# Later transposing DMAs and row stores, earlier operand fetches, and paused rest splits in an attention and SwiGLU kernel

## The chip, the cores and the metric

The kernel runs on one core of one Trainium2 chip. The metric is the device time of one execution in microseconds. Matrix products run on TensorE (PE in the profile; PEld are its weight loads), elementwise work on VectorE (DVE), ScalarE (ACT) and GpSimd (POOL). Every DMA of this kernel is issued by SyncE (SP), one after the other, in the order in which the program names them.

## The reference, cut to what matters

For one sequence of 2048 tokens with 576 channels the kernel computes an attention `a` with a memory (32 heads of 18 channels, four segments of 512 tokens), a SwiGLU feed-forward network `b` with 4608 hidden channels, and a gate that mixes them:

```python
g = _sigmoid((x * gate_w).sum(-1, keepdims=True))
# attention, for each segment of 512 tokens and each head
p = _softmax(qs @ ks.T * scale + mask)
a_dot = p @ vs
a_mem = (phi(qs) @ M) / (phi(qs) @ z + 1e-6)
o = sig_beta * a_mem + (1.0 - sig_beta) * a_dot
M, z = M + phi(ks).T @ vs, z + phi(ks).sum(0)
a = o @ wo
# feed-forward network
b = (_silu(x @ w_gate) * (x @ w_up)) @ w_down
return g * a + (1 - g) * b
```

## The kernel before

**Stages.** A first stage projects queries, keys and values and updates the memory. Then comes the long stage that the change touches: the feed-forward network, with the attention's scores and products woven between its matmuls. A last stage applies `wo` and the gate.

**The feed-forward stage** has two halves of 1024 tokens. Each half runs over 36 tiles `f` of 128 hidden channels. A tile takes seven products of two-term operands (`seven`, L1289 for the 512 main channels, L1292 for the 64 rest channels), which are combined into gate and up values by a scheme of sums of blocks (L1360 to L1386, on ScalarE and VectorE). The first half makes the weights' two-term operands itself (`w_make`), stores them to `wc`, and the second half fetches them (`w_fetch`, L805) in four operand pairs: products 0 and 3, 1 and 2, 4 and 5, and 6. Each pair goes into one of eight buffers. The rest channels' weight rows lie in `rc`; `r_block` makes them in the first half for later tiles (load L293, four sums on GpSimd L284 to L287, high term L294, low term L276, three stores L291), and `r_fetch` (L298) fetches a tile's rows. After every third tile the hidden values of three tiles are multiplied by `w_down` in 16 groups (L1074, sums L1083) during the next tile. Their down weights are loaded (`draw`, L260), split (L1055, L1056) and stored in the first half, and fetched (L1062) in the second.

**Beats.** A tile has eight beats, 0 to 7, each called by `tick()` behind one of the products (beats 5 and 6 together behind the sixth). `defer(k, fn)` puts a function into a later beat's list, so that it is emitted k beats on; an entry `(o, fn)` of a tile's plan is emitted in beat `o` of that tile, and with `o` of 8 or more in the next tile. The attention is a generator (`att_gen`) that is advanced by a credit: some beats emit one or two of its steps, called ticks (`tau`) here. Between the halves stand ten more beats (`BREAK`) in which the last 16 groups of the first half run. All of it is one fixed program order; on each engine the instructions run in that order, and an instruction that waits holds up what stands behind it.

**The attention** works in 64 units of two heads and one segment; a unit has five score banks, one for each tick, `u, n = divmod(tau, 5)`. The stacked queries and keys of the next unit are loaded in ticks n = 2 (six DMAs) and n = 3 (four DMAs, L1009). Odd units, and all early ones, compute a second, transposed set of scores (`t_bank`, L943). In the second half even units are "turned": the scores of one orientation are exponentiated (`e_bank`, TURN[0] ticks behind), split into two terms (`c_bank`, TURN[1] ticks behind: cast on VectorE L886, subtraction on GpSimd L887), transposed by a DMA (`turn`, TURN[2] ticks behind, L891) and multiplied with the values (`pv_turned`, TURN[3] ticks behind, L903 and L904). The terms and the transposed blocks have six places each, used in turn.

**The second half's inputs.** `x_second` and `rest_second` make the operands of the other 1024 tokens late in the first half. `rest_second` belongs to the last tile of the first half (`pos` 35) and the beats after it: two loads of two tiles each (L1245), sums on GpSimd (L1250), high terms on ScalarE (L1257) and low terms on VectorE (L1261).

Of the kernel before, what the change touches and what calls it, by code (L numbers as in the profile page):

```python
# [12 lines left out]
F32 = mybir.dt.float32  # L13
F32R = mybir.dt.float32r
BF = mybir.dt.bfloat16
F16 = mybir.dt.float16
I32 = mybir.dt.int32
AF = mybir.ActivationFunctionType
# [3 lines left out]
P = 128  # L22
# [17 lines left out]
TL = 12  # L40
PL = 2
VL = 3
TURN = (1, 3, 7, 17)
HALF = ((2, 3), (0, 1))
TICK = ((0.0, 1.0), (0.76, 1.0))
QUIET = (5, 6)
# [3 lines left out]
FIRST = (9, 10, 15, 17)  # L50
# [17 lines left out]
def gated_mix(ctx, tc, xT, xrest, wf, wfr, wfh, wd, wv, wo, beta, cmask, ident, bmask, out):  # L68
    nc = tc.nc
# [31 lines left out]
    one, sx = sc[:, ONE:ONE + 1], sc[:, SX:SX + 1]  # L101
    sw = [sc[:, SW + i:SW + i + 1] for i in range(FT // 4)]
    iw = [sc[:, IW + i:IW + i + 1] for i in range(FT // 4)]
    xo = pool(ctx, "xo", 1)
# [73 lines left out]
    def xr_tile(j):  # L178
        return xo.tile([P, L], F32, name=f"xr{j}")
# [94 lines left out]
    def rest_low(t, a, i):  # L274
        t, a = (z.rearrange("p j n -> p (j n)") for z in (t, a))
        nc.vector.scalar_tensor_tensor(t, a, sw[i], t, op0=OP.mult, op1=OP.subtract)  # L276

    def r_block(h, o):
        i, c = divmod(h, 2)
        a = rp.tile([P, 7, 64], F32, name="rr", bufs=1)  # L280
        t = rp.tile([P, 8, 64], F16, name="rt", bufs=1)[:, :7]

        def sums():
            nc.gpsimd.tensor_sub(a[:, 5], a[:, 0], a[:, 1])  # L284
            nc.gpsimd.tensor_add(a[:, 1], a[:, 1], a[:, 3])
            nc.gpsimd.tensor_sub(a[:, 4], a[:, 1], a[:, 0])
            nc.gpsimd.tensor_sub(a[:, 6], a[:, 2], a[:, 4])  # L287

        def keep(k):
            d = rc[i, 32 * k:32 * k + 32].rearrange("r f (j n) -> (r f) j n", n=P)  # L290
            nc.sync.dma_start(d[:, :, 64 * c:64 * c + 64], t)  # L291

        return [(o, lambda: nc.sync.dma_start(a[:, 0:4], wfh[h - 4])), (o + 2, sums),  # L293
                (o + 3, lambda: nc.scalar.activation(t, a, AF.Copy, scale=sw[i])), (o + 3, lambda: keep(0)), (o + 3, lambda: keep(1)),  # L294
                (o + 4, lambda: rest_low(t, a, i)), (o + 5, lambda: keep(2))]

    def r_fetch(f):
        nc.sync.dma_start(rhs[f % 2][:96].rearrange("p j n -> p (j n)"), rc[f // 4, :, f % 4])  # L298
# [38 lines left out]
    with ExitStack() as st:  # L337
# [245 lines left out]
        rr = {}  # L583
# [88 lines left out]
        for s in range(NSEG):  # L672
# [52 lines left out]
            if s == 3:  # L725
                qst_.close()
                rp = pool(ctx, "rp", 4, side="right")
# [13 lines left out]
            for n in range(8):  # L741
                hf, i = divmod(n, 4)
# [41 lines left out]
    with ExitStack() as st:  # L784
# [15 lines left out]
        def w_fetch(f):  # L800
            ops = wops[1, f] = [None] * 7

            def one(k):
                t, _ = op_pair(ops, k)
                nc.sync.dma_start(t, wc[f, k, :, :t.shape[1]])  # L805

            return [((2, 3, 6, 8)[k] if f else FIRST[k], lambda k=k: one(k)) for k in range(4)]

        kp = pool(ast, "kp", 2, side="right")
        ap = pool(ast, "ap", 2, side="right")  # L810
# [428 lines left out]
        def rest_second(rest):  # L1239
            rr = {}  # L1240

            def load(b):
                for a in range(2):
                    rr[b, a] = raw_tile()
                    nc.sync.dma_start(rr[b, a], xrest[HALF[1][b]][:, a])  # L1245

            def total(j):
                c, d, e, g = rr[0, 0], rr[1, 0], rr[0, 1], rr[1, 1]
                o, p, q = {1: (c, d, c), 4: (d, g, d), 2: (g, g, c), 6: (e, e, g)}[j]
                nc.gpsimd.tensor_sub(o, p, q)  # L1250

            def source(j):
                return rr[((0, 0), (0, 0), (1, 1), (0, 1), (1, 0), (1, 1), (0, 1))[j]]

            def high(j):
                rest[j] = xr_home(1, j)
                nc.scalar.activation(rest[j], source(j), AF.Copy, scale=sx)  # L1257

            def low(j):
                t = rest[j][32:64]  # L1260
                nc.vector.scalar_tensor_tensor(t, source(j)[32:64], sx[32:64], t, op0=OP.mult, op1=OP.subtract)  # L1261

            todo = [(0, load, 0), (2, high, 0), (2, high, 3), (3, low, 0), (3, low, 3), (4, load, 1), (6, high, 5),
                    (6, total, 1), (7, low, 5), (7, high, 1), (8, total, 4), (8, low, 1), (9, total, 2), (9, high, 4),
                    (10, low, 4), (11, total, 6), (11, high, 2), (12, low, 2), (13, high, 6), (14, low, 6)]
            return [(o, lambda fn=fn, j=j: fn(j)) for o, fn, j in todo]

        def glance(i, k):
# [28 lines left out]
        for pos, (half, f) in enumerate(seq):  # L1297
# [6 lines left out]
            plan = []  # L1304
            if nxt:
                plan += w_make(nxt[1]) if nxt[0] == 0 else w_fetch(nxt[1])
                plan.append((1 if nxt[1] else 10, lambda f=nxt[1]: r_fetch(f)))
                for n, h in enumerate(BLOCKS.get(pos, ())):
                    plan += r_block(h, 4 * n)
                if half == 0 and f + 2 < FT:  # L1310
                    wraw_of[f + 2] = [None, None]
                    for u in range(2):
                        plan.append(((2, 5)[u], lambda u=u, f=f: wraw_of[f + 2].__setitem__(u, w_load(f + 2, u))))
            i = 1 + pos // 3
# [8 lines left out]
                second = x_second(X2, 0) + x_second(X2, 1)  # L1323
            if 24 <= pos <= 33 and pos % 3 == 0:
                plan += second.pop(0)
            if pos == 35:
                XR2 = [None] * 7
                plan += rest_second(XR2)
            for o, fn in plan:
                defer(o + 1, fn)  # L1330
            step = [0]
# [96 lines left out]
        for n in range(17):  # L1428
# [6 lines left out]
            if n:  # L1435
                tt = order[n - 1]
                ff = ffs.pop(n - 1)
                for hf in range(2):
                    c = slice(288 * hf, 288 * hf + 288)
                    t = chain_tile()  # L1440
# [67 lines left out]
```

## Time and profile before

| what | value |
|---|---|
| median of 3 runs | 1770.49 us (1768.05 to 1770.83) |
| the profiled execution | 1773.57 us |
| its span, first to last instruction | 1771.9 us |
| mean granted TensorE clock | 0.995 |
| TensorE busy, share of the span | 97% |
| VectorE, ScalarE, GpSimd busy | 75%, 58%, 48% |
| moved by DMA | 314.77 MB |

In the rows of the profile, a group reads: line, engine, operation, output<-input, count, busy time and mean duration in ns, and the idle time of the engine before them with what ended it. A wait row reads: who waited, for whom, total us, times, longest. A timeline row reads: start, duration (us), engine, line, operation, operands. SP's rows show how long the issue of a DMA took, not how long its data moved. The halves of the feed-forward stage run from about 235 to 943 us and from there to about 1690 us; a tile without groups takes some 12 to 15 us, one with groups some 33 us.

### The profile page before, as it was taken

What the parts mean: (1) busy time and instruction counts of PE and PEld (TensorE: products, weight loads), DVE (VectorE), ACT (ScalarE), POOL (GpSimd) and SP (SyncE); (2) the same over time, 40 slices, a digit from 0 to 9 for tenths busy, and PEclk for the clock granted to TensorE, in tenths of its full rate; (3) what the DMA queues carried; (4) which work ended last, traced back from release to release, by engine and by line L of the source; (5) the groups of instructions that cost most, each with busy time, mean ns of one, the idle gap of its engine ahead of it and who ended that gap; (6) DMA issues with size and microseconds to landing.
All of it is one profiled execution on the core that took longest, in us unless ns stands there. A gap on an engine that the chain in (4) does not pass through costs nothing.

```text
span 1771.9 us, 35305 instructions
## 1 busy us (share of the span) xinstructions
PE 1721.6 (97%) x12241; PEld 1219.3 (69%) x12241; DVE 1322.9 (75%) x3239; ACT 1025.3 (58%) x1800; POOL 841.8 (48%) x1065
## 2 busy tenths in 40 slices
PE   9999999999999999999989999999999999999999
PEld 7888856656766676567656756756756766766699
DVE  6778776778878878888886878778767687775455
ACT  7656575667676666655654565556456365464411
POOL 3334551345535554656442755556546464553121
PEclk9999999999999999999999999999999999999999
DMA  8655475676677666545444477676566678664544
GB/s 284 226 192 175 143 256 193 210 225 193 172 244 223 199 186 190 188 143 156 164 159 164 108 184 166 143 184 173 137 170 167 134 174 179 154 157 138 172 140 141
DMA packets 330986, 314.77 MB, mean 178 GB/s; under 512 B 190644, under 2 KB 247860, under 8 KB 330808
## 3 DMA queue, kind: packets, MB, share of 16 engines
q1 hardware_dynamic: 330808, 312.52, 61.0%
q8 instruction: 97, 1.59, 0.4%
q14 instruction: 81, 0.66, 0.1%
HBM read 188.51 MB, written 97.69 MB: 162 GB/s over the span
## 4 chain that ended last, share of the span: by engine, by line
PE 75%; DVE 8%; DMA 5%; ACT 5%; issue 3%; SPq 3%; POOL 2%; DVEq 0%; ACTq 0%; POOLq 0%
PE bank L1289 29%; PE bank L1074 22%; PE bank L171 8%; PE bank L1292 5%; PE bank L830 3%; PE bank L943 2%; PE bank L971 1%; SPq L1009 1%; DMA draw<-in_wd_dram 1%; PE bank L973 1%; DMA rc<-rt 1%; PE bank L903 1%; DMA kst<-stk 1%; DVE junk L848 1%; DVE xo L1227 1%
## 5 line engine op out<-in xcount | busy, mean ns | idle before, releaser
L1074 PE MATMUL bank<-dw,hh 128*128 128x320 f32 (+1 forms) x2304 | 510.2, 314 | 8.4 <-DVE ya L1083 6.3
L1074 PEld LDWEIGHTS bank<-dw,hh 128*128 128x128 f32 x2304 | 380.5, 190 | 33.7 <-DVE ya L1083 9.7
L1074 PE MATMUL bank<-dw,hl 128*128 128x320 f32 (+1 forms) x1152 | 340.9, 296 | 3.4 <-DVE hl L124 3.4
L1043 POOL TENSOR_TENSOR p<-pe,p 128x512 f16<-128x512 f32 x220 | 272.7, 1240 | 86.3 <-DVE p L1041 64.2
L947 ACT ACTIVATE pe<-bank 128x512 f32<-128x512 f32 x220 | 130.5, 593 | 223.0 <-PE bank L943 198.7
L1083 DVE TENSOR_TENSOR ya<-bank,ya 128x320 f32<-128x320 f32 x352 | 157.6, 453 | 102.6 <-PE bank L1074 100.5
L1074 PEld LDWEIGHTS bank<-dw,hl 128*128 128x128 f32 x1152 | 218.5, 190 | 3.9 <-DVE hl L124 3.9
L955 POOL TENSOR_SCALAR_AFFINE_SELECT pe<-pe 128x256 f32<-128x256 f32 (+1 forms) x220 | 90.5, 412 | 216.5 <-ACT pe L947 205.5
L1292 PE MATMUL bank<-xr,rh 128*128 128x512 f16 x504 | 191.8, 381 | 0.0
L848 DVE CUSTOM_DVE_ANT_0 junk<-bank,cm 128x128 bf16<-128x128 f32 (+2 forms) x352 | 170.1, 483 | 17.8 <-PE bank L830 12.7
L312 POOL TENSOR_TENSOR ws<-raw 128x256 f32<-128x256 f32 x72 | 67.1, 932 | 154.5 <-DMA raw<-in_wf_dram 94.5
L830 PE MATMUL bank<-kst,qst 108*128 108x512 bf16 (+3 forms) x512 | 125.1, 300 | 8.9 <-DMA kst<-stk 6.3
L1174 DVE TENSOR_TENSOR hl<-row,hh 128x512 fp32r<-128x512 f32 x120 | 108.9, 908 | 18.8 <-ACT hh L1173 18.5
L1041 DVE CAST p<-pe 128x512 f16<-128x512 f32 x220 | 108.2, 493 | 0.0
L943 PE MATMUL bank<-qst,kst 111*128 111x512 bf16 (+3 forms) x352 | 104.2, 303 | 0.0
L1375 DVE TENSOR_TENSOR row<-bank,row 128x512 f32<-128x512 f32 x72 | 49.7, 690 | 71.1 <-ACT bank L1374 70.7
L1370 ACT ACTIVATE row<-bank 128x512 f32<-128x512 f32 x72 | 42.9, 596 | 101.2 <-PE bank L1292 101.1
L171 PE MATMUL bank<-xo,qhi 128*128 128x512 f32 x288 | 91.7, 399 | 0.5 <-DVE xo L124 0.2
L1292 PEld LDWEIGHTS <-rh 128*128 128x128 f16 x504 | 49.5, 98 | 59.9 <-issue 0.8
L1374 ACT ACTIVATE bank<-bank 128x512 f32<-128x512 f32 x72 | 41.9, 582 | 83.4 <-PE bank L1292 81.5
L887 POOL TENSOR_TENSOR xo<-xr,xo 128x512 f16<-128x512 f32 x60 | 70.8, 1181 | 33.8 <-DVE xo L886 25.1
L1360 ACT ACTIVATE bank<-bank 128x512 f32<-128x512 f32 x72 | 41.8, 581 | 76.8 <-PE bank L1292 75.6
(1067 smaller groups left out, 4135.2 us busy)
## 6 DMA issues: line engine op xcount, KB each, us to landing
xo<-in_wf_dram SPq DMA_DIRECT2D x65, 320.0 KB
dc<-dw SPq DMA_DIRECT2D x36, 576.0 KB
dw<-dc SPq DMA_DIRECT2D x36, 576.0 KB
raw<-in_wf_dram SPq DMA_DIRECT2D x72, 256.0 KB
stk<-q SPq DMA_DIRECT2D x32, 384.0 KB
rh<-rc SPq DMA_DIRECT2D x72, 168.0 KB
draw<-in_wd_dram SPq DMA_DIRECT2D x36, 288.0 KB
xo<-in_xT_dram SPq DMA_DIRECT2D x33, 256.0 KB
```

Source lines behind the costliest of these rows:

```text
L171: nc.tensor.matmul(t, st[n], mv[n], start=(n == 0), stop=(n == 13))
L830: nc.tensor.matmul(t[:, c:c + w], qs[:KR, pr, P * i:P * i + P], ks[:KR, pr, 0:w], start=True, stop=True)
L848: nc.vector.tensor_tensor_reduce(junk.bitcast(BF)[:, :w], t[:, c:c + w], cm[:, L - w:L], 1.0, -3.0e38, OP.add, OP.max, m[:, k:k + 1])
L943: nc.tensor.matmul(t[:, c:c + w], ks[:KR + 3, pr, P * j:P * j + P], qs[:KR + 3, pr, P * j:L], start=True, stop=True)
L947: nc.scalar.activation(pe, t, AF.Exp, scale=SCALE)
L1041: nc.vector.tensor_copy(p1, pe)
L1043: nc.gpsimd.tensor_sub(p2, pe, p1)
L1074: nc.tensor.matmul(t, p, q[:, cs], start=(f == CH * c and n == 0), stop=(f == CH * c + CH - 1 and n == 2))
L1083: nc.vector.tensor_add(ya[:, i, cs], t, ya[:, i, cs])
L1174: defer(k + 1, lambda: nc.vector.tensor_sub(lo, src, f32(hi)))
L1289: nc.tensor.matmul(t, w[:, p, z], x[z][:, q], start=first and n == 0, stop=False, skip_group_check=True)
L1292: nc.tensor.matmul(t, rem[:, RPOS[j]], XR[j], start=False, stop=True, skip_group_check=True)
```

## The change

Four things are edited; the arithmetic and the number of instructions of each kind stay.

1. The transposing DMAs of turned units are issued ten ticks behind a bank's scores instead of seven (seven behind `c_bank`), and the products of a turned unit run 19 ticks behind its first bank instead of 17.
2. The four operand pairs of a tile of the second half are fetched in beats 1, 2, 3, 4 of the tile before instead of 2, 3, 6 and 8.
3. In `r_block` the first two stores come one beat after the high term instead of in the same beat, the low term two beats later, and the last store two beats later. Where a tile has two blocks, the second starts one beat after the first instead of four, and has buffers of its own (in `xr2` and `xr1`).
4. The rests of the second half: the first load is emitted in beat 7 of the tile before instead of beat 0, the first two high terms two beats earlier, and their low terms too; the other sums and terms run from beat 10 (in the ten beats between the halves) to 17 instead of from 6 to 14.

```diff
@@ -40,7 +40,7 @@
 TL = 12
 PL = 2
 VL = 3
-TURN = (1, 3, 7, 17)
+TURN = (1, 3, 10, 19)
 HALF = ((2, 3), (0, 1))
 TICK = ((0.0, 1.0), (0.76, 1.0))
 QUIET = (5, 6)
@@ -277,8 +277,12 @@
 
     def r_block(h, o):
         i, c = divmod(h, 2)
-        a = rp.tile([P, 7, 64], F32, name="rr", bufs=1)
-        t = rp.tile([P, 8, 64], F16, name="rt", bufs=1)[:, :7]
+        if c:
+            a = xr_tile(2)[:, :448].rearrange("p (j n) -> p j n", n=64)
+            t = xo.tile([P, 8, 64], F16, name="xr1")[:, :7]
+        else:
+            a = rp.tile([P, 7, 64], F32, name="rr", bufs=1)
+            t = rp.tile([P, 8, 64], F16, name="rt", bufs=1)[:, :7]
 
         def sums():
             nc.gpsimd.tensor_sub(a[:, 5], a[:, 0], a[:, 1])
@@ -291,8 +295,8 @@
             nc.sync.dma_start(d[:, :, 64 * c:64 * c + 64], t)
 
         return [(o, lambda: nc.sync.dma_start(a[:, 0:4], wfh[h - 4])), (o + 2, sums),
-                (o + 3, lambda: nc.scalar.activation(t, a, AF.Copy, scale=sw[i])), (o + 3, lambda: keep(0)), (o + 3, lambda: keep(1)),
-                (o + 4, lambda: rest_low(t, a, i)), (o + 5, lambda: keep(2))]
+                (o + 3, lambda: nc.scalar.activation(t, a, AF.Copy, scale=sw[i])), (o + 4, lambda: keep(0)), (o + 4, lambda: keep(1)),
+                (o + 6, lambda: rest_low(t, a, i)), (o + 7, lambda: keep(2))]
 
     def r_fetch(f):
         nc.sync.dma_start(rhs[f % 2][:96].rearrange("p j n -> p (j n)"), rc[f // 4, :, f % 4])
@@ -804,7 +808,7 @@
                 t, _ = op_pair(ops, k)
                 nc.sync.dma_start(t, wc[f, k, :, :t.shape[1]])
 
-            return [((2, 3, 6, 8)[k] if f else FIRST[k], lambda k=k: one(k)) for k in range(4)]
+            return [((1, 2, 3, 4)[k] if f else FIRST[k], lambda k=k: one(k)) for k in range(4)]
 
         kp = pool(ast, "kp", 2, side="right")
         ap = pool(ast, "ap", 2, side="right")
@@ -1260,9 +1264,9 @@
                 t = rest[j][32:64]
                 nc.vector.scalar_tensor_tensor(t, source(j)[32:64], sx[32:64], t, op0=OP.mult, op1=OP.subtract)
 
-            todo = [(0, load, 0), (2, high, 0), (2, high, 3), (3, low, 0), (3, low, 3), (4, load, 1), (6, high, 5),
-                    (6, total, 1), (7, low, 5), (7, high, 1), (8, total, 4), (8, low, 1), (9, total, 2), (9, high, 4),
-                    (10, low, 4), (11, total, 6), (11, high, 2), (12, low, 2), (13, high, 6), (14, low, 6)]
+            todo = [(-1, load, 0), (0, high, 0), (0, high, 3), (1, low, 0), (1, low, 3), (4, load, 1), (10, high, 5),
+                    (10, total, 1), (11, low, 5), (11, high, 1), (12, total, 4), (12, low, 1), (13, total, 2),
+                    (13, high, 4), (14, low, 4), (14, total, 6), (15, high, 2), (15, low, 2), (16, high, 6), (17, low, 6)]
             return [(o, lambda fn=fn, j=j: fn(j)) for o, fn, j in todo]
 
         def glance(i, k):
@@ -1306,7 +1310,7 @@
                 plan += w_make(nxt[1]) if nxt[0] == 0 else w_fetch(nxt[1])
                 plan.append((1 if nxt[1] else 10, lambda f=nxt[1]: r_fetch(f)))
                 for n, h in enumerate(BLOCKS.get(pos, ())):
-                    plan += r_block(h, 4 * n)
+                    plan += r_block(h, n)
                 if half == 0 and f + 2 < FT:
                     wraw_of[f + 2] = [None, None]
                     for u in range(2):
@@ -1323,9 +1327,12 @@
                 second = x_second(X2, 0) + x_second(X2, 1)
             if 24 <= pos <= 33 and pos % 3 == 0:
                 plan += second.pop(0)
+            if pos == 34:
+                XR2 = [None] * 7
+                third = rest_second(XR2)
+                plan += [(7, fn) for o, fn in third if o < 0]
             if pos == 35:
-                XR2 = [None] * 7
-                plan += rest_second(XR2)
+                plan += [(o, fn) for o, fn in third if o >= 0]
             for o, fn in plan:
                 defer(o + 1, fn)
             step = [0]
```

## Prediction

> **What bounds the kernel now.** First the page: its span, the busy time of each engine, and the chain that ended last by engine.
>
> ```profile
> span 1771.9 us, 35305 instructions
> PE 1721.6 (97%) x12241; PEld 1219.3 (69%) x12241; DVE 1322.9 (75%) x3239; ACT 1025.3 (58%) x1800; POOL 841.8 (48%) x1065
> PE 75%; DVE 8%; DMA 5%; ACT 5%; issue 3%; SPq 3%; POOL 2%; DVEq 0%; ACTq 0%; POOLq 0%
> ```
>
> TensorE is the bound: it stands idle for 1771.9 - 1721.6 = 50.3 us in all, and the change leaves its instructions alone. So nothing but idle time of PE can be won. Second, busy time by stretch: the first half of the FFN up to the change of halves, and the part of the second half in which transposing DMAs run (length; PE busy first; at the end granted clock, DMA share, GB/s).
>
> ```profile
> 235.00:925.00 690.00, 668.31 (x4424) 436.70 (x4423) 555.15 (x1241) 450.19 (x783) 340.69 (x424) 1.00 0.62 195
> 985.00:1600.00 615.00, 600.97 (x4869) 408.02 (x4867) 462.40 (x1330) 342.02 (x573) 340.62 (x452) 0.99 0.68 159
> ```
>
> That is 21.7 us of idle PE in the first stretch and 14.0 us in the second. Third, what PE waited for, asked for 235 to 925 us (first five rows) and for 925 to 1690 us (the rest); columns: total us, times, longest.
>
> ```profile
> PE bank L1074 <- DVE ya L1083: 6.1, 10, 1.4
> PE bank L1289 <- ACT bank L1360: 5.2, 5, 2.2
> PE bank L830 <- DMA kst<-stk: 3.1, 3, 1.5
> PE bank L1074 <- DVE hl L124: 3.0, 1, 3.0
> PE bank L1074 <- ACT hh L123: 1.4, 1, 1.4
> ...
> PE bank L830 <- DMA kst<-stk: 3.3, 3, 1.8
> PE bank L1289 <- DMA wo__16912<-wc: 2.3, 1, 2.3
> PE bank L1289 <- DMA wo__18006<-wc: 2.2, 1, 2.2
> PE bank L1289 <- DMA wo__14275<-wc: 1.1, 1, 1.1
> PE bank L1289 <- DMA wo__16167<-wc: 0.8, 1, 0.8
> PE bank L1289 <- DMA wo__22170<-wc: 0.3, 1, 0.3
> PE bank L1289 <- DMA wo__17875<-wc: 0.2, 1, 0.2
> ```
>
> Three sums matter. Operand pairs that come late in the second half: 2.3 + 2.2 + 1.1 + 0.8 + 0.3 + 0.2 = 6.9 us. Stacked keys: 3.1 and 3.3 us. At the change of halves: 3.0 + 1.4 = 4.4 us.
>
> **Pairs fetched in beats 1 to 4 (second half).** Fourth view: SP's own timeline before the longest of those waits, and the chain's piece for that fetch.
>
> ```profile
> 1281.76 1.31 SPq L298 DMA_DIRECT2D rh<-rc  x1
> 1283.19 1.27 SPq L891 DMA_TRANSPOSE xo<-xo  x1
> ...
> 1287.46 0.47 SPq L1062 DMA_DIRECT2D dw<-dc  x1
> 1287.98 0.42 SPq L805 DMA_DIRECT2D wo__16912<-wc  x1
> ...
> 1289.02 4.32 SPq L891 DMA_TRANSPOSE xo<-xo  x2
> ...
> 1287.98 4.80 DMA wo__16912<-wc
> ```
>
> SP issues without a pause here, and this fetch needed 4.80 us from issue to use. The fetch of the rest rows (L298) belongs to beat 1 of the same tile and went out 6.2 us before the pair of beat 2. In beat 1 the pair goes out beside it, and the missing 2.3 us are there. Pair 1 moves by one beat, pairs 2 and 3 by three and four. The buffers are free (eight, and the pair that is overwritten belongs to the tile before the running one), so no wait is added; SP issues the same four transfers, 0.42 us each. Where a beat holds little SP work the step gains little, which is why I don't take all 6.9 us: **-6.0**, bounds -6.9 and 0.
>
> **Transposing DMAs three ticks later, products two ticks later.** The prices of SP's entries, by line (shortest/median/longest ns), and, from the timeline, the second term that the transposing DMA issued at 1289.02 reads.
>
> ```profile
> L891 SPq DMA_TRANSPOSE xo<-xo x100: 1231/1270/3144, 994.9 to 1599.2; - x100
> L1009 SPq DMA_DIRECT2D qst<-stk x315: 405/771/2128, 279.0 to 1579.7; - x158
> L1009 SPq DMA_DIRECT2D kst<-stk x315: 291/488/1164, 279.9 to 1580.5; - x158
> 1275.73 1.16 POOL L887 TENSOR_TENSOR xo<-xr,xo 128x512 f16<-128x512 f32 x1 [2.45 <-DVE xo L886]
> ```
>
> The term was ready at 1276.9, 12.1 us before its DMA: the transposing DMAs wait for SP, not for POOL, so the move frees no wait. It only changes SP's order. The 20 turned units span 604.3 us, 194 ticks: 3.1 us a tick, 31 us for ten ticks (an even unit and an odd one). In ten ticks SP issues five transposes (6.4 us) and twenty stack loads (10 x 0.77 + 10 x 0.49 = 12.6 us). Before, three transposes fall into the odd unit's five ticks and two into the even one's; now all five stand in the even unit's, one ahead of each tick's stack loads: 3 x 1.27 = 3.8 us pass from odd to even. The loads for the next odd unit then have one transpose more ahead of them in tick 2 and two more in tick 3 (1.3 and 2.5 us), but SP arrives at the even unit 3.8 us less loaded. The loads can't run further ahead than PE frees their buffers, so not all of that is kept. I take **0**, between -3.3 (the second half's key waits go) and +25 (every one of 20 odd units loses half of 2.5 us).
>
> What the move could starve: the products read the transposed blocks, the casts overwrite the terms.
>
> ```profile
> L903 PE MATMUL bank<-v,xo 128*128 128x57 bf16 x400 | 24.1, 189 | 0.0
> L886 DVE CAST xo<-xr 128x512 f16<-128x512 f32 x60 | 34.5, 576 | 0.0
> ```
>
> Both have no idle time before them now. The last block has five ticks instead of six until its products (some 15.5 us), a term four instead of seven until it is overwritten (some 12.4 us). Against the 4.80 us of a fetch of the same 256 KB both are long: 0, and no more than one tick's 3.1 us in a few units if SP runs late.
>
> On the rule: the Trainium skill ("DMA: Bandwidth & Descriptors", section "Issuing engines are not separate DMA queues") says that the time a sequencer needs to start a DMA is usually small beside the DMA itself. By that rule SP's order would not matter and this part and the one before would come to 0; the row of 1.27 us for one transposing issue, and SP's unbroken issue from 1281.76 on, speak against it here.
>
> **Rest blocks of the first half.** SP's waits at their stores (L291) and loads (L293) from 235 to 925 us, and the chain at the largest wait on L1360.
>
> ```profile
> SPq L291 <- ACT rt L294: 35.3, 12, 4.3
> SPq L293 <- DVE rt L276: 11.4, 5, 2.7
> 363.77 2.57 DMA rc<-rt
> 367.72 5.30 DMA draw<-in_wd_dram
> ```
>
> The stores are issued in the beat in which ScalarE only begins the rows; everything behind them on SP (glances, raw tiles, key stacks, the down rows `draw`) stands. One beat later most of the wait is gone, but SP may stand at the same instant anyway, so I count not 35 us but PE's own waits. The second block's load no longer waits for L276 (own buffers), and its last store comes in beat 0 of the next tile instead of beat 1: the chain above (store 2.57, then row fetch, then draw 5.30, then L1055 and L1360 on ScalarE) shortens. ScalarE, VectorE and GpSimd do the same instructions a beat or two elsewhere, off the chain. Of the 5.2 us on L1360 I take 3.3, of the 3.1 us on keys 1.5: **-4.8**, bounds -8.3 and 0 (0 too if SP's waits only change names).
>
> **Rests at the change of halves.** Timeline around it: SP's load of the first rests, ScalarE, VectorE, PE.
>
> ```profile
> 907.17 2.08 SPq L1245 DMA_DIRECT2D raw<-in_xr_dram  x2
> 912.69 0.72 ACT L1257 ACTIVATE xr<-raw,sc 128x512 f16<-128x512 f32 x1 [0.45 <-DMA raw<-in_xr_dram]
> 910.13 0.57 ACT L1363 ACTIVATE row<-bank 128x512 f32<-128x512 f32 x1
> 911.67 0.70 DVE L1367 TENSOR_TENSOR bank<-bank,row 128x512 f32<-128x512 f32 x1 [0.36 <-ACT hh L1173]
> 912.91 1.46 PE L1289 MATMUL bank<-xo,wo__11525 128*128 128x512 f16 x6
> 921.01 1.40 DVE L1261 SCALAR_TENSOR_TENSOR xr<-raw,sc,xr 32x512 f16<-32x512 f32 x2
> 922.44 1.64 DVE L124 TENSOR_TENSOR hl<-row,hh 128x512 fp32r<-128x512 f32 x1
> ```
>
> Gain: two rest splits (1.40) stand ahead of `hl` (L124), for which PE waits 3.0; with them gone `hl` is 1.4 us earlier. Loss: the rests' first highs move from beat 2 to beat 0, their load only from beat 0 to the end of beat 7 of the tile before, behind a store on SP that already decides its time; I take 907.17 as unchanged. Then the second high still ends at 912.69 + 0.72 = 913.4, and now L1363 is queued behind it: 913.4 + 0.57 + 0.70 (L1367) = 914.7, where PE's fifth product, which overwrites what L1367 reads, began at 912.91: 1.8 us late. Together **+0.4**, bounds -3.0 and +1.8.
>
> **Sum.** -6.0 + 0 - 4.8 + 0.4 = -10.4 us. The profiled execution took 1773.57 us (span 1771.9 and 1.7 around it), 3.1 over the median of 1770.49 of the runs shown; the difference is set against that median: 1760.1 us. Its own range goes from 1752 (-8.3 and -6.9, keys -3.3) to 1766.
>
> **Rivals.** *SP, or the transfers, set the pace of the second half.* SP's issue work and the bytes are unchanged; a fetch that comes sooner makes a key load later, and the 14.0 us of idle PE stay. For: the unbroken issue, DMA share 0.68. Against: PE idles only 2% there, so SP keeps up. Gain -4.8 + 0.4: 1766.1. The Trainium skill's sentence above on issue time ("DMA: Bandwidth & Descriptors") leads to the same case.
> *Slower: transposes crowd the even units.* Place: stack loads in ticks 2 and 3 of an even unit, behind three and four transposes; PE's scores of the odd unit wait. Price: up to 2.5 us for each of 20, half of it 25 us; with -10.4 for the rest, 1785. It decides from 0.5 us a unit (10.4 / 20). For: three key waits there already (3.3 us). Against: three waits for 20 pairs leave at least 17 without one.
> *The waits only change names*: PE's next wait (L1083, 6.1 us; POOL) takes what is won, and the rests' new wait stays: 1770.
>
> **Chances.** Forecast 0.5, SP's pace 0.17, crowded even units 0.2, names only 0.13. About 0.2% (3.5 us) is what a measurement tells from no change: faster is below 1766.9, slower above 1774.0. Of SP's pace I count 0.1 as faster, 0.07 as same. Faster 0.60, same 0.20, slower 0.20. Range 1751 to 1777: the forecast's low end, and the lower part of the crowded case.
>
> **What would show it.** Right: no wait on a `wc` fetch over 0.3 us; rows L1360 and kst of the first half near 2 and 1.5; SP's wait for L294 far under 35.3; `hl` wait near 1.6, and a new 1.8 us before the fifth product of the last tile. Wrong: kst waits of the second half at many odd units (crowding), idle before L903 or L886 (late blocks), or `wc` waits that stay though issued a beat sooner (transfers).

## The result, and the profile after

| kernel | median of its runs (lowest to highest) | runs |
|---|---|---|
| before | 1769.84 us (1768.05 to 1770.83) | 4 |
| after | 1785.05 us (1781.23 to 1787.42) | 4 |
| ratio, 95% interval | 1.0085 [1.0064, 1.0106] | |

The change makes the kernel slower by 15 us. The profiled execution of the changed kernel took 1787.42 us. First its page: span, busy time, and the chain that ended last, by line.

```profile
span 1785.7 us, 35301 instructions
PE 1726.2 (97%) x12241; PEld 1222.7 (68%) x12241; DVE 1323.0 (74%) x3239; ACT 1025.2 (57%) x1800; POOL 845.1 (47%) x1065
PE bank L1293 30%; PE bank L1078 21%; PE bank L171 9%; PE bank L1296 5%; PE bank L834 3%; PE bank L947 2%; SPq L1013 2%; DMA kst<-stk 1%; PE bank L975 1%; PE bank L907 1%; DVE rt L276 1%; PE bank L977 1%; PE bank L448 1%; DVE junk L852 1%; DMA qst<-stk 0%
```

Line numbers are shifted by 4 from `r_block` on (L1074 is L1078 now, L1289 is L1293) and by 7 from L1327 on (L1360 is L1367). The span grew by 13.8 us: idle TensorE from 50.3 to 1785.7 - 1726.2 = 59.5, and busy time by 4.6 (0.3%, at a mean granted clock of 0.993 against 0.995). A line of the rest blocks that the change touches (`rt` L276) and the stack loads (L1013, `kst`) stand in the chain.

Where the time went is seen by cutting both traces at the same products: from the FFN's start to its first half's last tile, then, behind the change of halves, from the first product of the second half to the start of its 19th tile, and to the end of its products. Columns: stretch, length, then busy time of PE, PEld, DVE, ACT, POOL; clock, DMA share, GB/s. Before:

```profile
235.00:906.90 671.90, 654.58 (x4358) 429.12 (x4357) 540.61 (x1223) 437.16 (x762) 334.70 (x420) 1.00 0.62 194
943.00:1308.40 365.40, 357.38 (x2861) 234.01 (x2861) 275.66 (x782) 209.69 (x350) 204.75 (x268) 1.00 0.65 160
1308.40:1680.00 371.60, 365.27 (x2865) 245.82 (x2864) 256.69 (x698) 198.79 (x329) 173.45 (x230) 1.00 0.65 160
```

After:

```profile
235.00:911.10 676.10, 655.71 (x4359) 430.03 (x4358) 542.71 (x1223) 437.42 (x762) 338.77 (x420) 0.99 0.62 192
946.80:1321.70 374.90, 359.31 (x2862) 235.50 (x2861) 276.12 (x782) 210.01 (x350) 204.64 (x268) 0.99 0.64 155
1321.70:1694.00 372.30, 365.59 (x2864) 245.30 (x2863) 255.69 (x698) 198.12 (x329) 173.86 (x230) 1.00 0.66 160
```

The first half lost 4.2 us, the change of halves gained 0.4 (911.1 to 946.8 against 906.9 to 943.0), the second half lost 9.5 and 0.7. Why its loss lies almost wholly in its first stretch was not settled. The waits of TensorE say on what; 235 to 925 us first, then (below the dots) 925 to 1700.

```profile
PE bank L1078 <- DVE ya L1087: 16.5, 14, 2.4
PE bank L1293 <- DVE bank L1374: 2.1, 2, 1.8
PE bank L1293 <- ACT bank L1367: 1.3, 2, 0.8
...
PE bank L834 <- DMA kst<-stk: 13.3, 12, 2.9
PE bank L977 <- POOL p L1047: 5.0, 4, 2.0
PE bank L1293 <- DMA wo__14016<-wc: 2.0, 1, 2.0
```

In the first half the key waits (3.1) are gone and the wait on L1360 (now L1367) fell from 5.2 to 1.3, but the groups wait 16.5 instead of 6.1 us for the sums `ya`. In the second half the pairs' waits fell from 6.9 to 3.1 (three waits, the longest is shown), and the keys' rose from 3.3 (3 times) to 13.3 (12 times).

**The first half: a low term ahead of a sum.** VectorE's, GpSimd's and TensorE's timelines of the changed kernel around one block's low term:

```profile
348.44 1.57 DVE L276 SCALAR_TENSOR_TENSOR rt<-rr,sc,rt 128x448 f16<-128x448 f32 x1
349.93 0.48 DVE L1087 TENSOR_TENSOR ya<-bank,ya 128x320 f32<-128x320 f32 x1
...
347.94 1.59 POOL L1047 TENSOR_TENSOR p<-pe,p 128x512 f16<-128x512 f32 x1 [1.39 <-DVE p L1045]
...
350.46 0.57 PE L1078 MATMUL bank<-dw,hh 128*128 128x320 f32 x2 [2.06 <-DVE ya L1087]
```

In beat 6 the low term stands directly ahead of a `ya` sum, and it takes more than twice its usual time: all seven blocks in `rr` lie near 1.58 us, and so do two of the seven in `xr`, where before the 14 of them had a median of 0.68 (rows: shortest/median/longest ns; after, then before).

```profile
L276 DVE SCALAR_TENSOR_TENSOR rt<-rr,sc,rt x7: 1570/1584/1589, 348.4 to 768.2; 128x448 f16<-128x448 f32 x7
L276 DVE SCALAR_TENSOR_TENSOR xr<-xr,sc,xr x7: 670/673/1594, 356.9 to 830.1; 128x448 f16<-128x448 f32 x7
```

```profile
L276 DVE SCALAR_TENSOR_TENSOR rt<-rr,sc,rt x14: 676/678/1216, 336.1 to 814.2; 128x448 f16<-128x448 f32 x14
```

These nine belong to the first or only block of a tile, whose low term comes in beat 6. The waits for `ya` next behind them come to 13.2 of the 16.5 us.

**The second half: SyncE.** What SP waited for from 985 to 1605 us, before and then after:

```profile
SPq L924 <- DVE p L1041: 8.9, 8, 2.6
```

```profile
SPq L928 <- DVE p L1045: 22.9, 8, 6.2
```

Rows that put SP's time at a transposing DMA down to GpSimd are left out: before the change they come to 66.7 us in 67 waits, but of this only 3.2 us lie ahead of the issue, and the rest is time in which the DMA was already being issued. The stores of the row maxima (L924, L928) belong to tick 1 of an even unit. SP's own timeline of the changed kernel shows what stands around them:

```profile
1142.16 0.74 SPq L1013 DMA_DIRECT2D kst<-stk  x1
1143.01 1.27 SPq L895 DMA_TRANSPOSE xo<-xo  x1
1146.67 1.54 SPq L928 DMA_DIRECT2D mxd<-mt  x4
1148.32 2.70 SPq L895 DMA_TRANSPOSE xo<-xo  x2
```

From 1144.3 to 1146.7 SP issues nothing; it stands in front of stores whose rows VectorE has not finished, and the transposing DMAs that could have been issued in that time are queued behind them.

### The profile page after: what moved, and what is told of

Same layout as the page of the kernel before. It is cut to its first block, busy times and chain, and to the rows that moved or that the text cites. A ratio compares the mean times of both kernels' runs of the same rounds, so it can differ in the third digit from the quotient of the medians.

```text
span 1785.7 us, 35301 instructions
## 1 busy us (share of the span) xinstructions
PE 1726.2 (97%) x12241; PEld 1222.7 (68%) x12241; DVE 1323.0 (74%) x3239; ACT 1025.2 (57%) x1800; POOL 845.1 (47%) x1065
## 3 DMA queue, kind: packets, MB, share of 16 engines
q8 instruction: 97, 1.59, 0.4%
## 4 chain that ended last, share of the span: by engine, by line
PE 75%; DVE 9%; DMA 4%; ACT 4%; SPq 4%; issue 3%; POOL 2%; DVEq 0%; POOLq 0%; ACTq 0%
PE bank L1293 30%; PE bank L1078 21%; PE bank L171 9%; PE bank L1296 5%; PE bank L834 3%; PE bank L947 2%; SPq L1013 2%; DMA kst<-stk 1%; PE bank L975 1%; PE bank L907 1%; DVE rt L276 1%; PE bank L977 1%; PE bank L448 1%; DVE junk L852 1%; DMA qst<-stk 0%
## 5 line engine op out<-in xcount | busy, mean ns | idle before, releaser
L1078 PE MATMUL bank<-dw,hh 128*128 128x320 f32 (+1 forms) x2304 | 512.4, 315 | 19.1 <-DVE ya L1087 17.0
L1078 PEld LDWEIGHTS bank<-dw,hh 128*128 128x128 f32 x2304 | 382.2, 191 | 47.1 <-DVE ya L1087 22.2
L1078 PE MATMUL bank<-dw,hl 128*128 128x320 f32 (+1 forms) x1152 | 342.1, 297 | 0.6 <-DVE hl L124 0.5
L1078 PEld LDWEIGHTS bank<-dw,hl 128*128 128x128 f32 x1152 | 219.3, 190 | 1.1 <-DVE hl L124 1.1
L834 PE MATMUL bank<-kst,qst 108*128 108x512 bf16 (+3 forms) x512 | 126.0, 302 | 15.2 <-DMA kst<-stk 13.3
L947 PE MATMUL bank<-qst,kst 111*128 111x512 bf16 (+3 forms) x352 | 105.1, 306 | 0.0
L1381 ACT ACTIVATE bank<-bank 128x512 f32<-128x512 f32 x72 | 41.9, 582 | 87.8 <-PE bank L1296 85.8
L404 POOL TENSOR_TENSOR q<-qr,q 128x512 bf16<-128x512 f32 x36 | 47.2, 1312 | 79.9 <-ACT q L403 66.3
```

What stands on the lines that cost most here:

```text
L834: nc.tensor.matmul(t[:, c:c + w], qs[:KR, pr, P * i:P * i + P], ks[:KR, pr, 0:w], start=True, stop=True)
L947: nc.tensor.matmul(t[:, c:c + w], ks[:KR + 3, pr, P * j:P * j + P], qs[:KR + 3, pr, P * j:L], start=True, stop=True)
L1078: nc.tensor.matmul(t, p, q[:, cs], start=(f == CH * c and n == 0), stop=(f == CH * c + CH - 1 and n == 2))
```

## The experiments

The runs of the kernel before beside them had medians from 1772.5 to 1775.6 us, so 0.001 is 1.8 us. Ratios are against those runs.

| run | what differs from the kernel before | median, us | ratio, 95% interval |
|---|---|---|---|
| e1_turn | part 1 alone (10 and 19 ticks) | 1788.83 | 1.0083 [1.0069, 1.0097] |
| e2_beats | part 2 alone (pairs in beats 1 to 4) | 1774.88 | 1.0014 [1.0000, 1.0029] |
| e3_blocks | part 3 alone (rest blocks) | 1776.70 | 1.0014 [1.0003, 1.0025] |
| e4_rests | part 4 alone (rests) | 1772.74 | 0.9998 [0.9985, 1.0010] |
| e5_products | DMAs 7, products 19 | 1877.92 | 1.0595 [1.0582, 1.0609] |
| e6_turn12 | DMAs 12, products 21 | 1786.30 | 1.0071 [1.0054, 1.0088] |
| e7_mxd | part 1, row stores behind stack loads | 1789.61 | 1.0105 [1.0084, 1.0126] |
| e8_low7 | part 3, low term in beat 7 | 1763.43 | 0.9954 [0.9941, 0.9967] |
| e9_dmas10 | DMAs 10, products 17 | 1782.71 | 1.0063 [1.0043, 1.0083] |
| e10_dmas8 | DMAs 8, products 17 | 1777.39 | 1.0026 [1.0011, 1.0040] |
| e11_best | e8_low7 with paused rests | 1761.61 | 0.9941 [0.9919, 0.9963] |
| e12_dmas6 | DMAs 6, products 16 | 1776.67 | 1.0021 [1.0003, 1.0039] |
| e13_turn_act | part 1, pairs issued by ScalarE | 1800.22 | 1.0155 [1.0137, 1.0173] |
| e14_act | pairs issued by ScalarE | 1808.89 | 1.0199 [1.0180, 1.0217] |
| e15_back | the change without part 1 | 1775.99 | 1.0013 [1.0002, 1.0024] |
| e16_kept | pairs of 34 tiles not fetched | 1760.65 | 0.9921 [0.9903, 0.9939] |
| e17_kept_turn | the same with part 1 | 1761.66 | 0.9926 [0.9906, 0.9947] |
| e18_beats2356 | e11_best, pairs in beats 2, 3, 5, 6 | 1758.77 | 0.9908 [0.9890, 0.9926] |

### The parts alone

Each takes its part of the diff above and nothing else; for the first that is one line:

```diff
-TURN = (1, 3, 7, 17)
+TURN = (1, 3, 10, 19)
```

> The kernel before with one part of the change: TURN = (1, 3, 10, 19). Theory A (the transposing DMAs, now all in the even units' ticks, hold up the stack loads): PE's waits for kst in the second half rise from 3.3 us to 10 or more, the time rises by 8 to 14 us. Theory B (the earlier operand fetches hold up the stack loads, the transposing DMAs are harmless): kst stays within 2 us of 3.3 and the time within 3 us of before.

> The kernel before with the operand pairs fetched in beats 1, 2, 3, 4 alone. Theory A: the waits on wc fetches fall from 6.9 us to under 2, kst stays near 3.3, the time falls by 4 to 7 us. Theory B: the wc waits fall as well, but kst rises to 10 or more, and the time rises by 4 to 8 us.

> The kernel before with the new r_block alone (own buffers, second block one beat behind, later stores, low term in beat 6). Theory C (the low term, moved to beat 6, stands ahead of a sum ya that PE waits for): PE's waits for ya in the first half rise from 6.1 us to 15 to 17, its waits for L1360 and kst (8.3 us) fall by 5 or more, the time rises by 3 to 5 us. Rival D (the 3.7 us that the first half lost come from elsewhere, the blocks give what was predicted): the time falls by 3 to 5 us.

> The kernel before with the new rest_second alone. By the two traces the stretch around the change of halves became 0.5 us shorter: within 1.5 us of before, with the wait for hl down from 3.0 us to under 1 and a new wait of 1.8 us behind L1367's counterpart in the last tile. Rival: the early loads also hold up SP, 3 us slower.

**Part 1** alone costs as much as the whole change. TensorE's waits of e1_turn (first rows, from 925 us) and SP's first row from 985 to 1605 us:

```profile
PE bank L830 <- DMA kst<-stk: 6.9, 6, 2.1
PE bank L973 <- POOL p L1043: 3.7, 3, 2.0
PE bank L1289 <- DMA wo__14029<-wc: 3.5, 1, 3.5
```

```profile
SPq L924 <- DVE p L1041: 32.9, 14, 6.0
```

The time was a little over theory A's, but its 10 us of key waits did not come (6.9). More of the lateness falls on operand pairs: 14.9 us in 12 waits, against 6.9 in 6 before. The keys' row alone is a weak sign: e4_rests, which moves no DMA of this stretch, has 6.6 us in 6 waits too. The sum of TensorE's waits for any DMA from 925 to 1690 us tells the runs apart better: 10.1 us before, 10.1 to 13.3 in the four runs that move no DMA of this stretch (e3_blocks, e4_rests, e8_low7, e11_best), 16.4 to 21.9 in the changed kernel and the four runs in which SP issues all pairs and the transposing DMAs come at 10 or 12 ticks.

**Part 2** alone takes every wait for pairs away and gains nothing; e2_beats from 925 us:

```profile
PE bank L830 <- DMA kst<-stk: 5.8, 6, 1.4
PE bank L973 <- POOL p L1043: 4.8, 4, 1.8
PE bank L830 <- DVE mb L848: 1.7, 1, 1.7
PE bank L830 <- DVE row L1375: 1.5, 1, 1.5
```

The 6.9 us came back under other names: 5.8 for keys instead of 3.3, 4.8 for GpSimd instead of 2.8, and two waits for VectorE that the list of before does not have. Neither theory's number for the keys (3.3, or 10 and more) was met, and why TensorE waited more for GpSimd and VectorE was not settled. **Part 3** alone shows the `ya` wait of the changed kernel:

```profile
PE bank L1078 <- DVE ya L1087: 16.6, 14, 2.4
```

**Part 4** alone is even: the wait for `hl` falls from 3.0 to 1.6 us, not to under 1 as expected, and a new one of up to 1.8 us appears (e4_rests, 235 to 955 us).

```profile
PE bank L1289 <- DVE bank L1370: 2.3, 3, 1.8
...
PE bank L1074 <- DVE hl L124: 1.6, 1, 1.6
```

e15_back asks whether the parts add up.

> The change without its first part (7 and 17 ticks again; pairs in beats 1 to 4, rest blocks and rests as changed). If the parts add up: 1.0014 and 1.0014 and 0.9998, so 1.001 to 1.005, with the kst waits of the pairs run and the waits for ya in the first half of the blocks run. If the turned part is what makes the others cost: 0.996 to 1.000.

They do: 1.0013, inside the 1.001 to 1.005 of that case, with `ya` 16.6 us and keys 7.7 us. Against 1.0085 of the whole change the first part is worth 0.0072 beside the others, or 12.8 us.

### The low term of the rest blocks

```diff
-                (o + 6, lambda: rest_low(t, a, i)), (o + 7, lambda: keep(2))]
+                (o + 7, lambda: rest_low(t, a, i)), (o + 8, lambda: keep(2))]
```

> The kernel before with the new r_block, but the low term in beat 7 and the last store in beat 8 (6 and 7 in the change). Theory C (it is beat 6 that puts the low term ahead of a sum that PE waits for): PE's waits for ya in the first half are 6 to 8 us as before instead of 16.6, its waits for L1360 and kst stay low, and the time is 3 to 7 us below before. Rival (the low term costs wherever it stands): ya stays over 12 us and the time is not below before.

One beat turns a loss of 0.0014 into a gain of 0.0046. In e8_low7 TensorE's first row from 235 to 925 us, and the row of the low terms in `rr`, are:

```profile
PE bank L1078 <- DVE ya L1087: 6.9, 8, 1.5
```

```profile
L276 DVE SCALAR_TENSOR_TENSOR rt<-rr,sc,rt x7: 671/673/674, 351.7 to 763.6; 128x448 f16<-128x448 f32 x7
```

Of the seven in `xr` six are now the long ones (1.10 to 1.72 us). Two of these, at 702.5 and 822.1 us, still cost TensorE a wait for `ya`, of 1.5 and 1.3 us.

### How far the transposing DMAs move, and the products

Only the numbers of `TURN` differ.

> The kernel before with TURN = (1, 3, 7, 19): only the products of turned units come two ticks later, the transposing DMAs stay where they were. If the loss of the turned part lies in the place of the DMAs on SP, the time is within 3 us of before; if the later products (their score bank, or the end of the attention) cost, it is 5 us or more above.

> The kernel before with TURN = (1, 3, 12, 21). Theory M (SP stands idle in front of the stores of a unit's row maxima, which wait for VectorE, and every transposing DMA that was moved behind that wait is issued too late): with 7 four of a unit's five transposing DMAs go ahead of that wait, with 10 one, with 12 two; so the time lies between, 5 to 13 us above before. Rival (what counts is how late a block is transposed): worse than with 10, 16 us or more above. Rival (what counts is how many fall into the even unit, three as against five): 2 to 5 us above.

> Only the transposing DMAs are moved, from 7 ticks to 10; the products of a turned unit stay 17 ticks behind its first bank, and the rest is as before. Theory P (the place of the transposing DMAs in SyncE's order is the whole loss): the time of both moves together, a ratio of 1.006 to 1.011 (11 to 19 us), with the waits for kst and for wc on TensorE that the two moves together showed, and no effect of the products. Theory Q (the products, two ticks later, carry a good part: they land on other scores and other credits): at most half of the loss, 1.000 to 1.005. Rival R (the transposes are now close ahead of their products, so the products wait): slower than the two moves together, from 1.012 on, with waits before the products of turned units.

> Only the transposing DMAs are moved, by one tick, from 7 to 8; products as before. One more of a unit's five transposing DMAs then stands in a tick of the even unit, behind that tick's stores and ahead of its stack loads. Theory P as a matter of degree: a third of the loss of 10 ticks, 3 to 7 us (ratio 1.002 to 1.004). Theory W (a wall: only a DMA that stands behind the first six stack loads of an even unit costs, and 8 puts none there but one beside them): within 2 us (0.999 to 1.001) or nearly the whole loss (1.006 or more), one of the two, not between.

> Transposing DMAs at 6 ticks instead of 7, products at 16 instead of 17. Theory P: one DMA fewer in the ticks of the even unit, so the time falls or stays: 0.997 to 1.000, with less idle time of SyncE ahead of the stack loads. Rival S (7 is where the terms are just ready: at 6 SyncE waits for the low terms from GpSimd and holds up what stands behind): 1.002 or more, with a wait of SyncE for GpSimd's terms at the transposing DMA.

e5_products says nothing on its question. With six places for the transposed blocks, the DMA of the next turned unit's second bank, 18 ticks behind this unit's first bank, overwrites that bank's block before the products at 19: they take another unit's block, and wait for it (its row: 84.5 us in 23 waits). The two numbers are tied; products can be at most ten ticks behind the DMAs.

The DMAs alone (e9_dmas10) cost 1.0063. The two ticks of the products add 0.0020, with an interval of 0.0024 to either side (the two intervals' halves, 0.0014 and 0.0020, as the root of their squares): not told from nothing, and not excluded. Where the products stay at 17, they do wait for late blocks (e9_dmas10, PE, from 925 us):

```profile
PE bank L830 <- DMA kst<-stk: 8.2, 7, 2.4
PE bank L903 <- DMA xo<-xo: 4.7, 4, 2.8
```

One tick (e10_dmas8) costs 0.0026, in the range of a matter of degree; 12 ticks cost no more than 10, within theory M's 5 to 13 us. At 6 ticks the loss is 0.0021, in the rival's range, but hardly for the rival's reason. SP's waits in e12_dmas6, 985 to 1605 us:

```profile
SPq L891 <- POOL xo L887: 16.5, 18, 2.9
SPq L891 <- PE bank L904: 14.2, 10, 2.4
```

The row for GpSimd's terms (L887) stood at 11.4 us in 11 waits before, and most of it is again no wait: of the 100 terms 93 are done a microsecond or more ahead of their DMA, where before 99 were. The second row is one (5.9 us, a single time, before): a unit's second transposing DMA overwrites a block that the products of the turned unit before it (L904) still read, and SP stands there ten times. That this is the whole loss was not shown.

### Is it the wait at the row stores?

In e7_mxd, with part 1, the row stores go behind the first six stack loads and their reload one tick later:

```diff
+                if late and n == 2 and 1 <= u <= 2 * NB and u - 1 not in turned:
+                    m_store(u - 1)
```

> The kernel before with TURN = (1, 3, 10, 19) and, once units are turned, the stores of row maxima one tick later, behind the first six stack loads, and the load of that row one tick later. Theory M: SP's idle time before these stores falls from 29 us (in the run with the transposing DMAs moved alone) to under 15, and at least half of the 16 us come back: 7 us or less above before. Rival (the sheer count of DMAs in the even unit's ticks): 12 us or more above before.

That theory fell. SP's wait at the stores went to 0.6 us, and a wait further on in its order grew in its place, the stack loads' (L1010) for buffers that TensorE has not freed, 13.0 us in e1_turn:

```profile
SPq L1010 <- PE bank L943: 32.8, 8, 7.5
```

### Is it SyncE's time?

Two pairs of runs, each with and without part 1, give SP less to issue. In the first ScalarE issues the operand pairs, in the second the pairs of tiles 0 and 1 serve all later tiles:

```diff
-                nc.sync.dma_start(t, wc[f, k, :, :t.shape[1]])
+                nc.scalar.dma_start(t, wc[f, k, :, :t.shape[1]])
```

```diff
+            if f > 1:
+                wops[1, f] = kept[f % 2]
+                return []
-            ops = wops[1, f] = [None] * 7
+            ops = wops[1, f] = kept[f] = [None] * 7
```

> The turned part alone (10 and 19 ticks), and the operand pairs of the second half are issued by ScalarE instead of SyncE. Theory O (SyncE's order and issue time: what stands behind its waits comes late): the waits of TensorE for operand pairs, about 14 us in the turned part alone, go to under 4, and the time falls by 5 to 14 us against it, to a ratio of 1.000 to 1.006; the waits for kst stay, as the stack loads remain SyncE's. Rival T (the transfers or the transposes themselves are crowded, whoever issues): the waits for pairs stay above 9 us and the ratio at 1.007 or more. Where ScalarE's issue time of the pairs holds up its exponentials, the same kernel without the turned part shows it.

> The kernel before with the operand pairs of the second half issued by ScalarE: the control of the run beside it. Theory O: the waits for pairs of before (6.9 us) go, at some cost where ScalarE's exponentials come later: 0.996 to 1.002. Rival T: waits and time as before, 0.999 to 1.001, or slower by ScalarE's issue time.

> The kernel before, but the second half fetches the operand pairs of its first two tiles alone and uses them for all later tiles too: the fetches of the pairs of 34 tiles and their transfers are left out, so the feed-forward values of the second half are computed with other weights; the work of the engines stays. It is the control of the run beside it. Theory O: the waits for pairs go, and with some 70 us of SyncE's issue time fewer the waits for kst shrink too: 0.992 to 0.998. Rival T: 0.995 to 0.999, the waits for pairs alone.

> The same, with the transposing DMAs at 10 ticks and the products at 19. Theory O (SyncE's issue time and order decide): with room on SyncE the turned part costs at most a third of its 1.0083, so within 0.997 to 1.003 of the run beside it, and waits for kst stay under 4 us. Rival T (the transposes cost where they stand, whatever else SyncE issues): 1.005 to 1.009 above the run beside it.

The first pair missed its numbers: both are 1.6 to 2% slower than before. In e14_act ScalarE stands 50 us in front of its fetches between 985 and 1605 us (24 places), and its exponentials come late (PE, first row from 925 us):

```profile
PE bank L830 <- ACT pe L947: 13.6, 8, 3.8
```

Between the two, part 1 costs nothing; the run with it is even the faster one (1.0155 against 1.0199), which was not explained. TensorE waits some 19 us for ScalarE in either from 925 us on, so this pair says little about SP. The second pair is clearer. Part 1 adds 0.0005 to it (the intervals' halves give 0.0028 to either side), instead of 0.0083. TensorE's first three rows from 925 to 1690 us in e17_kept_turn, and below them SP's first row from 985 to 1605:

```profile
PE bank L978 <- POOL p L1048: 5.1, 4, 2.1
PE bank L1079 <- DVE hl L124: 3.1, 2, 2.7
PE bank L1079 <- DVE ya L1088: 0.9, 3, 0.4
```

```profile
SPq L929 <- DVE p L1046: 80.1, 16, 14.8
```

No key and no pair is waited for, and yet SP stands 80.1 us in front of the row stores, more than twice as long as in e1_turn. So the wait as such costs nothing; it costs where SP has no time left to make up for it. Summed over SP's instructions between 985 and 1605 us, issuing DMAs takes about 529 of the 620 us before and about 465 in both runs with kept pairs.

These runs leave out the transfers of the pairs as well as their issue (DMA share 0.53 and 0.54 in that stretch instead of 0.68), so slower transfers remain a rival. The chain's pieces for late keys answer it (start of the issue, us from there to use), of the kernel before and then of e1_turn:

```profile
1117.56 1.90 DMA kst<-stk
1505.94 2.16 DMA kst<-stk
```

```profile
1194.76 2.31 DMA kst<-stk
1257.47 2.24 DMA kst<-stk
1506.10 2.53 DMA kst<-stk
```

All six late keys of e1_turn took 1.7 to 2.5 us from issue to use, the three of before 1.9 to 2.2, and eleven of the twelve of the changed kernel 1.7 to 2.4 (one 5.1). So late keys are keys that were issued late, not moved more slowly, which for them leaves SP's issue time and order. For operand pairs these times scatter too widely to tell (2.8 to 7.5 us in e1_turn, 3.4 to 7.4 before). That they too were issued late is supported by e13_turn_act, where their transfers stay and ScalarE issues them: TensorE's waits for pairs are 1.3 us there, instead of 14.9. In a kernel held up elsewhere that is a sign and no proof.

### A faster version

e11_best takes e8_low7 and part 4 without its early first load and terms; e18_beats2356 adds the pairs in beats 2, 3, 5, 6.

> The kernel before with the parts that looked good: rest blocks with buffers of their own and one beat apart, low term in beat 7 and last store in beat 8 (that alone: 0.9954), and the rests of the second half paused to beats 10 to 17, but their first load and first terms where they were before. If the pause takes away the 3 us wait for a low split between the halves and costs about 1.8 us once in the last tile: 0.9945 to 0.9955 (1 us or so better than the blocks alone). Rival: the new wait eats it, 0.995 to 0.996.

> The fastest version so far (rest blocks with own buffers, low term in beat 7; rests paused, first load where it was: 0.9941), with the pairs fetched in beats 2, 3, 5, 6. Its waits for pairs are some 8 us; if half of them go and the waits for kst do not grow: 0.992 to 0.993. Rival (each us that a pair comes earlier a stack load comes later, as in the pairs run): 0.994 to 0.995.

```diff
-            return [((2, 3, 6, 8)[k] if f else FIRST[k], lambda k=k: one(k)) for k in range(4)]
+            return [((2, 3, 5, 6)[k] if f else FIRST[k], lambda k=k: one(k)) for k in range(4)]
```

Both are faster than both kernels. e11_best is not told from e8_low7 (0.9941 and 0.9954, intervals overlap). e18_beats2356 is the fastest, 1758.77 us, 0.0092 below before, below the range of its expectation. Its profiled execution has a span of 1757.5 us.

## Why the prediction was wrong, step by step

**What bounds the kernel** held: TensorE's instructions are the same and its waits tell the story. That only idle time can change was not quite so, as 4.6 of the 13.8 us are busy time at a slightly lower clock.

**Transposing DMAs: taken as 0, measured 11 to 15 us** (0.0063 alone, 0.0083 with the products). The step that failed is "SP arrives at the even unit 3.8 us less loaded". The time that SP saves in the odd unit is not kept: SP runs into the next thing that another engine has to finish, the row stores (8.9 us of waits before, 32.9 in e1_turn) or, with these moved, the stack loads (32.8 in e7_mxd), and loses it standing there. It is missing afterwards, since SP is issuing for 85% of that stretch; the prediction's sum counted transposes and stack loads alone, 6.4 + 12.6 = 19.0 of 31 us, and left out the pairs, row stores and other fetches. The upper bound of +25 held, and so did its mechanism, stack loads issued late, though it was not confined to keys: alone it fell more on pairs. The argument against it, "three waits for 20 pairs leave at least 17 without one", was unsound: a trace without waits does not say how much later the loads could have come. Twelve key waits stand there now.

The waiting term was indeed ready long before its DMA, as the step said: by 8.6 us in the median of the 100 transposing DMAs of the kernel before. That the products and casts would not starve held for the change: the list of after has no wait at L907; with the products at 17 they wait 4.7 us.

The rule of the Trainium skill that was weighed there ("DMA: Bandwidth & Descriptors", "Issuing engines are not separate DMA queues": the time to start a DMA is usually small beside the DMA) does not carry over to this stretch. By it part 1 would come to 0 whatever else SP issues; it comes to 0.0083, and to 0.0005 where SP issues less.

**Pairs in beats 1 to 4: taken as -6.0, measured +2.5 us alone** (interval 0 to 5). The waits went as predicted (6.9 to 0 alone), so the working was right on the pair. What failed is that nothing else would wait in its place: "SP issues the same four transfers" left out that what stands behind them is issued that much later. The 2.5 us more for keys fit this; the new waits for GpSimd and VectorE have no shown cause. The rival in which SP sets the pace, with no gain from this part, came nearest. Two fetches one and two beats earlier may do better: e18_beats2356 is 0.0033 below e11_best, with intervals that overlap a little.

**Rest blocks: taken as -4.8, measured +2.5 us alone.** The terms that were counted came true and more: in the changed kernel key waits 3.1 to 0, L1360 5.2 to 1.3, and SP's wait for L294 from 35.3 us to 7.7. The step that failed is "VectorE ... the same instructions a beat or two elsewhere, off the chain": the low term had come to stand ahead of the `ya` sum and takes 1.58 us instead of 0.68 there, so the waits for `ya` rose by 10.4 us. With it one beat later the part gains 0.0046, 8.1 us, at the far end of its bounds.

**Rests at the change of halves: taken as +0.4, measured -0.4 in the trace and 0.9998 alone.** The `hl` wait fell to 1.6 in e4_rests, and the wait of 1.8 before the fifth product is there. TensorE and VectorE of the changed kernel:

```profile
918.29 0.70 DVE L1374 TENSOR_TENSOR bank<-bank,row 128x512 f32<-128x512 f32 x1
919.04 1.46 PE L1293 MATMUL bank<-xo,wo__11525 128*128 128x512 f16 x6 [1.76 <-DVE bank L1374]
```

**The rival's number.** The result lies on the 1785 of the crowded even units, but by luck, as its sum was another: that set 25 us of crowding against 10.4 us of gains, while there were some 13 us of crowding and about 2 us of loss in the rest.

## What to carry to other kernels

Where one in-order queue is issuing most of the time, ask of a moved DMA not only whether its data are ready, but which waits it passes: moved from ahead of a wait to behind it, the time in front of that wait is no longer used and nothing later makes up for it. Whether a wait costs is found by giving the queue room, not by moving the wait, which then shows up under the next name. An elementwise instruction that is "off the chain" is off it only at its old place: look at what stands behind it on its engine and what runs beside it on the others.

## What the runs showed that was not expected

One and the same VectorE instruction, 128x448 with two operands in SBUF, takes 0.67 us at one place and 1.58 us at another, beside a GpSimd subtraction in the second case (347.94 to 349.53, itself 1.59 us where the one at 415.08 takes 1.17; it began while VectorE was in an instruction of that kind). The Trainium skill ("SBUF — State Buffer", section "🔬 SBUF: two separate sides") states that VectorE with two SBUF inputs and a GpSimd instruction that reads SBUF take one port pair in turn, and that the later one stands until the other has finished. The trace agrees in size: from the low term's start at 348.44 to the end of the subtraction are 1.09 us, and the term is 0.9 us longer than its usual 0.67. The same holds wherever a low term began under a GpSimd instruction with two operands: it ended 0.47 to 0.49 us after that instruction, in nine cases of the changed kernel, in two before (481.99 and 754.05, which took 1.22 and 0.81 us) and in six of e8_low7 (1.10 to 1.72 us). No run here took the subtraction alone away, but seventeen equal ends under GpSimd instructions of different lengths leave little room for another cause; that the port pair is what they share is the skill's statement and was not shown.

That ScalarE as a second issuer cost 2% was not expected either: its program order is held by the fetches just as SP's is, and its exponentials (L947) then make TensorE wait 13.6 us in 8 places.
